# Squared-ReLU attention and feed-forward on one core: first batch split at 128 queries, score bursts joined behind v products, w_out sums on two engines

## The chip, the core and the metric

The kernel runs on one NeuronCore of a Trainium2 chip. Its engines work side by side, each through its own list of instructions in a fixed order, and wait for each other by semaphores: TensorE (matmuls and transposes, PE in the profile; PEld is its weight loads), VectorE (DVE), ScalarE (ACT), GpSimd (POOL) and SyncE (SP, which here only starts DMAs). TensorE writes to PSUM; VectorE and ScalarE carry results from there to SBUF; GpSimd works from SBUF to SBUF and also starts some DMAs. The metric is the device time of one execution in microseconds, as a median over runs.

## The reference

Attention with a squared ReLU in place of the softmax, for 8 batches, 12 heads, 448 positions and 64 dimensions a head, and then a feed-forward layer with a squared ReLU on the 3584 tokens:

```python
scores = scale * np.matmul(q, k.transpose(0, 1, 3, 2))
attn = np.maximum(scores, 0.0) ** 2 / S
attn_out = np.matmul(attn, v)
x = np.ascontiguousarray(attn_out.transpose(0, 2, 1, 3)).reshape(B * S, H * D)   # 3584 x 768
h = x @ w_in                                                                      # 768 x 2048
r = np.maximum(h, 0.0)
g = r * r
return (g @ w_out).astype(np.float32)                                             # 2048 x 768
```

## The kernel before

**Units and rounds.** A unit `n` is four heads of one batch: three units a batch, 24 in all. The 448 positions are seven groups of 64, and a round is one key group `t` of one unit. For each round four 64x64-tiled matmuls (`scores`, L379) give the scores of 448 queries against 64 keys for the unit's four heads, in a PSUM tile `sp` of which there are two. `square` carries them on in two passes: relu with a scale, PSUM to `rel` (VectorE L405 or ScalarE L408), then the square, `rel` to `at` in fp16 (ScalarE L412 or GpSimd L414). When the seven rounds of a unit are there, `av` multiplies by v (28 tiled matmuls, L442) into two `mm` banks (of four), and a copy (L462, L464) writes x, turned, so that model dimensions lie on partitions (`xt`).

**Feed-forward.** `h_mms` (L503) takes 128 columns of w_in as the weights and streams x past them, six matmuls for each of the 16 blocks of 128 rows of h; `evac_g` squares h on ScalarE (L492) and zeroes it where h was not positive on VectorE (L487). The product with w_out goes in groups of matmuls of 384 columns: the first batch partly in plain groups (`plain_groups`, L595), the rest by a Strassen-like scheme of seven products for eight (`o_groups`, L657), which needs sums of g blocks (`combine`, L636, VectorE) and sums of w_out blocks (`combine_w2`, L621): t1, t2, t4 and t3, each in two halves of 1536 elements, all on GpSimd, with the planned time 60 us as the earliest.

**The start.** Batch 0 is cut by queries, `PARTS`: 256 and 192. The scores of the first 256 queries come first, for pairs of rounds in one score tile, with their v products; then `h_pair` computes h for two blocks of 128 rows with the 256 queries, while the scores of the other 192 follow. q and k of units 0 to 5 are turned by TensorE transposes (`turn_pe`, L319), later ones by DMA transposes (`turn_dma`, L334). Loads of v, w_in and w_out go through GpSimd's DMA queue (L348, L353, L358), q and k mostly through SP's (L277). Where TensorE has nothing ready before the planned time 45 us, the planner puts in dummy matmuls (`fill`, L794).

**The order.** Nothing in the code runs in the order in which it stands. Every operation goes into a list (`plan.add`, `plan.pe`) with the engines that could do it, their costs, what it depends on, the buffers it needs and a due time. `Plan.run` then plays this list through with these costs, lets each engine take the ready operation with the earliest due time (`pick`), and so fixes each engine's order of instructions when the program is built. On the chip only the order and the true dependences are left, not the planned times. In the steady part the main loop adds two rounds of scores as one operation (a score pair, eight matmuls), now and then a v product (`avs`), and then h and w_out groups by a credit of time (`run_some`). A change between 64x64 tiles and full 128x128 matmuls has a cost in the planner (`SWITCH`).

Of the kernel before, what the change touches and what calls it, by code (L numbers as in the profile page):

```python
# [27 lines left out]
class Op:  # L28
    def __init__(self, alts, deps, bufs, due, after, mode):
        self.alts = alts  # L30
        self.bufs = bufs
        self.due = due
        self.after = after
        self.mode = mode
        self.fixed = due is not None
        self.nexts: list = []
        self.deps = [d for d in deps if d is not None]
        self.engine = None
        self.start = self.end = 0.0


class Plan:
# [29 lines left out]
    def run(self):  # L72
# [19 lines left out]
        mode, dma, done = None, 0.0, 0  # L92
        while done < n_ops:
# [6 lines left out]
            while again:  # L100
                again = False
                for eng in ("PE", "ACT", "DVE", "POOL", "SP"):
                    if self.busy[eng] > now + 1e-9:
                        continue
                    got = self.pick(eng, now, waiting)
# [10 lines left out]
                    if eng == "PE":  # L116
                        begin += self.SWITCH.get((mode, op.mode), 0.0)
# [38 lines left out]
        return max(op.end for op in self.ops)  # L156

# [35 lines left out]
def kernel(  # L193
# [117 lines left out]
    def turn_pe(n, w, cast, at=None):  # L311
        op, blk, view = cast
        ps, to = Buf("mm"), Buf("qkt")

        def flip():
            flat = ps.tile.bitcast(FP16)
            for t in range(TJ):
# [3 lines left out]
        def copy(fn):  # L321
            return lambda: fn(to.tile.rearrange("p t c -> p (t c)"),
                              ps.tile.bitcast(FP16)[:, 0:TJ * P])

        pe = plan.pe(0.4, flip, [op], [blk, ps], at=at)
        done = plan.add([("DVE", 0.55, 0.62, copy(nc.vector.tensor_copy)),
                         ("ACT", 0.82, 0.91, copy(nc.scalar.copy))], [pe], [ps, to],
                        due=plan.now + 0.3)
        qkt[n, w] = done, to

    def turn_dma(n, w, cast):
# [3 lines left out]
            out=to.tile, in_=blk.tile.rearrange("p t c -> p (t c)")))], [op], [blk, to])  # L335
        qkt[n, w] = done, to
# [26 lines left out]
    PARTS = slice(0, 4 * TP), slice(4 * TP, S)  # L363
    WHOLE = slice(0, S)

    def scores(rounds, bufs, cols, joint, at=None):
# [4 lines left out]
        def emit():  # L371
            for j, (n, t) in enumerate(rounds):
                qT, kT = qkt[n, "q"][1].tile, qkt[n, "k"][1].tile
                sp, c0 = (bufs[0].tile, j * w) if joint else (bufs[j].tile, 0)
                for e in range(2):
                    for f in range(2):
# [10 lines left out]
        return plan.pe(0.000424 * w * len(rounds), emit, [x[0] for x in turned],  # L387
                       bufs + [x[1] for x in turned], "tile", at)
# [34 lines left out]
    def av(n, ts, cols=WHOLE, at=None):  # L423
# [3 lines left out]
        joint = w < S and u == 1  # L427
        c0 = w if joint else 0
# [20 lines left out]
        op = plan.pe(0.000424 * w * len(ts), emit, [z[0] for z in used] + [vst[n][0]] + before,  # L449
                     [z[1] for z in used] + [vst[n][1]] + banks, "tile", at)  # L450
        av_ops.setdefault(n, []).append(op)
        if ts[-1] < TJ - 1 or (w < S and u == 0):
            return
        for f in range(2):
            def put(kind, f=f):
                def run():
                    dst, src = x.tile[:, 2 * u + f, cols], banks[f].tile[:, 0:w]
                    if joint:
                        dst = x.tile[:, f:f + 3:2, cols]
                        src = banks[f].tile[:, 0:2 * w].rearrange("p (u c) -> p u c", c=w)  # L460
# [6 lines left out]
            n_el = 2 * w if joint else w  # L467
            xt_ops.setdefault((b, cols.start), []).append(plan.add(
                [act(n_el, put("ACT")), dve(n_el, put("DVE"))], av_ops[n][-1:],
                [banks[f], x], due=plan.now + 0.2))  # L470

# [47 lines left out]
    def h_pair(f, cols, at=None):  # L519
        w = cols.stop - cols.start  # L520
        cost = max(0.1, 0.000424 * w) * NM
        cell: list = []

        def half(z):
            def run(at=None):
                gts.setdefault(0, Buf("g"))
                if not cell:
                    cell.append(Buf("mm"))
                op = plan.pe(cost, h_mms(cell[0], 0, f + z, cols, z * w),
                             xt_ops[0, cols.start] + [w1_ops[(f + z) // 4]] + cell[1:],  # L530
                             [cell[0], xts[0]], at=at)
                cell.append(op)
                if z:
                    evac_g(op, cell[0], 0, [f, f + 1], cols)
            return run

        return [(cost, half(z)) for z in range(2)]

    def store(op, places, cols, osb):
# [5 lines left out]
        for i, (b, t) in enumerate(places):  # L545
            ways = [("SP", 0.56, 3.0, emit(nc.sync, i, b, t))]
            if ending and len(fifo) < 7:
                ways.append(("ACT", 0.56, 3.0, emit(nc.scalar, i, b, t)))
# [62 lines left out]
    def combine_w2():  # L611
# [5 lines left out]
        for name, args, before in steps:  # L617
# [3 lines left out]
                           nc.gpsimd.tensor_sub(*args(r)))],  # L621
                         [w for hf in range(2) for w in w2_ops[hf]]
                         + [t_ops[x][z] for x in before]
                         + (plain_ops if name == "t3" else []), after=60.0)
# [115 lines left out]
    def push_dense(b):  # L740
        if b:
            hs = [h_group(b, f) for f in range(NF)]
        else:
            hs = list(first_h) + [z for f in range(0, NF, 2) for z in h_pair(f, PARTS[1])]
# [31 lines left out]
    NPE = 6  # L776
    ROUNDS = NUN * TJ
# [32 lines left out]
    w1_ops = [load_w1(0, 1.4, 1.4)]  # L810
    load_v(2, 1.4, 1.5)
# [4 lines left out]
    turn_pe(0, "k", casts[0, "k"], 5.8)  # L816
    turn_pe(0, "q", casts[0, "q"])
    rounds = [divmod(r, TJ) for r in range(STREAM)]
    tiles = [(part, rounds[r:r + 2]) for part in range(2) for r in range(0, STREAM, 2)]
    NA = len(tiles) // 2  # L820
    turns = {1: (1, "k"), 2: (1, "q"), 3: (2, "k"), 4: (2, "q")}
    first_h = deque(z for f in range(0, NF, 2) for z in h_pair(f, PARTS[0]))
# [8 lines left out]
    def some_h(count):  # L831
        for _ in range(count):
            first_h.popleft()[1]()

    def tile(i, at=None):
        part, rs = tiles[i]
# [11 lines left out]

    for i in range(NA):
        tile(i, 7.6 + 1.1 * i)  # L850
        if i >= 2:
            put(0, tiles[i - 2][1])
        if i in turns:
            n, w_ = turns[i]
            turn_pe(n, w_, casts[n, w_])
    tile(NA)
    put(0, tiles[NA - 2][1])
    tile(NA + 1)
    put(0, tiles[NA - 1][1])
# [8 lines left out]
    for i in range(NA + 2, 2 * NA):  # L868
        tile(i)
        if (i - NA) % 2:  # L870
            some_h(2)
        if i == NA + 8:
            put(1, rounds[0:2 * TJ])
            some_h(1)
    for w_ in "kq":
        turn_pe(3, w_, casts[3, w_])
    some_h(1)
    put(1, rounds[2 * TJ:])
    some_h(len(first_h))
# [4 lines left out]

# [67 lines left out]
```

## Time and profile before

| | |
|---|---|
| median of 7 runs | 394.09 us (392.44 to 394.46) |
| the profiled execution | 393.74 us, of it 392.0 us from the first to the last instruction (the span) |
| mean granted TensorE clock | 0.996 of full |
| TensorE h, 448 columns (L503) | 672 matmuls |
| TensorE w_out products (L657) | 208 + 208 + 176 + 88 + 32 + 16 matmuls of 384 columns |
| ScalarE squares (L412, 896 elements) | 104, mean 953 ns |
| GpSimd squares (L414, 896 elements) | 43, mean 1680 ns |
| GpSimd w_out sums (L621) | 8, mean 3083 to 3116 ns |
| dummy matmuls (L794) | 52 |
| w_in blocks (L353) | 4 DMAs, 768 KB each, median 13.4 us from issue to landing |

Read it so: the span is one execution on the hardware's profiler, in microseconds from its first instruction; a group is the instructions of one line and one shape, with the time its engine was busy with them and the mean time of one. Matmuls overlap, so the sum over a group is best taken from start to start in the timeline.

### The profile page before, as it was taken

What the parts mean: (1) busy time and instruction counts of PE and PEld (TensorE: products, weight loads), DVE (VectorE), ACT (ScalarE), POOL (GpSimd) and SP (SyncE); (2) the same over time, 40 slices, a digit from 0 to 9 for tenths busy, and PEclk for the clock granted to TensorE, in tenths of its full rate; (3) what the DMA queues carried; (4) which work ended last, traced back from release to release, by engine and by line L of the source; (5) the groups of instructions that cost most, each with busy time, mean ns of one, the idle gap of its engine ahead of it and who ended that gap; (6) DMA issues with size and microseconds to landing.
All of it is one profiled execution on the core that took longest, in us unless ns stands there. A gap on an engine that the chain in (4) does not pass through costs nothing.

```text
span 392.0 us, 8414 instructions
## 1 busy us (share of the span) xinstructions
PE 381.8 (97%) x3344; PEld 200.7 (51%) x3344; DVE 256.0 (65%) x362; ACT 278.8 (71%) x409; POOL 194.5 (50%) x179
## 2 busy tenths in 40 slices
PE   8999999999799999999999999999999999999995
PEld 4567765444355444544454444544545445555563
DVE  2876664476694678676886576865796567455941
ACT  3987899997866687788886787587787776244221
POOL 8577498899857574463433443175432344000100
PEclk9999999999899999999999999999999999999999
DMA  9999999962677774866397486674183001210152
GB/s 191 195 224 271 281 235 165 272 128 89 105 159 215 179 167 77 194 161 135 65 215 172 107 208 130 174 164 79 37 112 82 0 2 47 56 40 3 27 134 82
DMA packets 69671, 52.72 MB, mean 134 GB/s; under 512 B 36864, under 2 KB 69632, under 8 KB 69632
## 3 DMA queue, kind: packets, MB, share of 16 engines
q1 hardware_dynamic: 53744, 38.61, 39.0%
q0 software_dynamic: 15296, 12.72, 22.4%
q10 hardware_dynamic: 592, 0.85, 0.6%
q8 instruction: 26, 0.43, 0.4%
q14 instruction: 13, 0.11, 0.1%
HBM read 45.61 MB, written 11.01 MB: 144 GB/s over the span
## 4 chain that ended last, share of the span: by engine, by line
PE 79%; POOL 7%; ACT 5%; issue 3%; DVE 3%; DMA 1%; SPq 0%; DVEq 0%; POOLq 0%; ACTq 0%
PE mm L503 31%; PE mm L657 29%; PE sp L379 8%; PE mm L442 7%; POOL wt L621 3%; ACT at L412 2%; ACT rel L408 2%; POOL w L621 1%; DMA raw<-in_q_dram 1%; PE mm L794 1%; PE mm L791 1%; DVE rel L405 1%; DVE comb L636 1%; PE mm L319 1%; POOL at L414 1%
## 5 line engine op out<-in xcount | busy, mean ns | idle before, releaser
L503 PE MATMUL mm<-xt,w 128*128 128x448 f16 (+2 forms) x864 | 156.5, 332 | 0.8 <-DVE g L487 0.8
L414 POOL TENSOR_TENSOR at<-rel 128x896 f16<-128x896 f32 (+1 forms) x47 | 78.0, 1662 | 78.6 <-DVE rel L405 71.9
L503 PEld LDWEIGHTS <-w 128*128 128x128 f16 x864 | 79.5, 98 | 71.0 <-issue 15.2
L405 DVE TENSOR_SCALAR rel<-sp 128x896 f32<-128x896 f32 (+3 forms) x85 | 91.8, 1088 | 35.1 <-PE sp L379 27.2
L487 DVE SCALAR_TENSOR_TENSOR g<-mm,g 128x448 f16<-128x448 f32 (+2 forms) x128 | 79.0, 621 | 54.0 <-ACT g L492 53.5
L412 ACT ACTIVATE at<-rel 128x896 f16<-128x896 f32 (+2 forms) x111 | 103.3, 943 | 3.7 <-PE mm L442 1.0
L492 ACT ACTIVATE g<-mm 128x448 f16<-128x448 f32 (+2 forms) x128 | 69.1, 546 | 42.2 <-PE mm L503 40.6
L408 ACT ACTIVATE rel<-sp 128x896 f32<-128x896 f32 (+2 forms) x84 | 76.4, 912 | 12.8 <-PE sp L379 10.3
L300 POOL CAST blk<-raw 128x896 f16<-128x896 f32 x42 | 40.2, 965 | 52.0 <-issue 26.2
L657 PEld LDWEIGHTS <-comb 128*128 128x128 f16 x416 | 38.9, 98 | 32.7 <-issue 5.0
L379 PE MATMUL sp<-qkt,qkt 64*64 64x448 f16 (+2 forms) x756 | 50.3, 339 | 2.2 <-ACT rel L408 1.8
L579 ACT ACTIVATE part<-mm 128x384 f32<-128x384 f32 x46 | 22.5, 488 | 38.5 <-PE mm L657 38.3
L669 DVE SCALAR_TENSOR_TENSOR part<-mm,part 128x384 f32<-128x384 f32 x52 | 28.5, 553 | 25.9 <-ACT part L579 17.7
L657 PE MATMUL mm<-wt,comb 128*128 128x384 f16 x208 | 37.2, 327 | 0.5 <-DVE comb L636 0.5
L657 PE MATMUL mm<-w,comb 128*128 128x384 f16 x208 | 36.8, 326 | 0.0
L442 PE MATMUL mm<-at,vs 64*64 64x448 f16 (+1 forms) x672 | 35.0, 341 | 1.4 <-DVE g L487 1.4
L657 PEld LDWEIGHTS <-g 128*128 128x128 f16 x264 | 25.2, 99 | 20.9 <-issue 5.3
L657 PE MATMUL mm<-w,g 128*128 128x384 f16 x176 | 31.1, 326 | 0.0
L379 PEld LDWEIGHTS <-qkt 64*64 64x64 f16 x756 | 15.5, 105 | 29.1 <-issue 27.9
L348 POOL DMA_DIRECT2D vs<-in_v_dram x48 | 29.9, 627 | 0.4 <-DMA g<-in_q_dram 0.4
L442 PEld LDWEIGHTS <-vs 64*64 64x64 f16 x756 | 20.7, 107 | 15.4 <-issue 5.0
L561 POOL COPY rest<-g 128x1024 f16<-128x1024 f16 x8 | 9.9, 1239 | 31.8 <-DVE g L487 31.8
(48 smaller groups left out, 221.2 us busy)
## 6 DMA issues: line engine op xcount, KB each, us to landing
out_dram<-part SPq DMA_DIRECT2D x108, 96.0 KB, 2.2
raw<-in_k_dram SPq DMA_DIRECT2D x22, 448.0 KB, 4.5
raw<-in_q_dram SPq DMA_DIRECT2D x21, 448.0 KB, 4.9
vs<-in_v_dram POOLq DMA_DIRECT2D x48, 112.0 KB, 4.0
w<-in_moe_w_in_dram POOLq DMA_DIRECT2D x4, 768.0 KB, 13.4
w<-in_moe_w_out_dram POOLq DMA_DIRECT2D x4, 768.0 KB, 18.1
qkt<-blk SPq DMA_TRANSPOSE x36, 3.3
raw<-in_q_dram ACTq DMA_DIRECT2D x1, 448.0 KB, 4.9
```

The costliest lines, as they stand in the source:

```text
L300: return lambda: fn(blk.tile.rearrange("p t (f d) -> p f t d", f=2), tile_of().rearrange("p f (t d) -> p f t d", d=D))
L348: nc.gpsimd.dma_start(out=buf.tile[64 * r:64 * r + 64], in_=src[:, u, hs])
L379: nc.tensor.matmul(sp[64 * c:64 * c + 64, e, c0:c0 + w].rearrange("p (t c) -> p t c", c=TP), lhsT=kT[r, t, 64 * e:64 * e + 64], rhs=qT[r, ...
L405: dve(n, lambda: nc.vector.tensor_scalar(out=rel(), in0=sp.tile[:, :, 0:width], scalar1=0.0, scalar2=SK, op0=ALU.max, op1=ALU.mult)),
L408: act(n, lambda: nc.scalar.activation(out=rel(), in_=sp.tile[:, :, 0:width], func=AF.Relu, scale=SK))],
L412: act(n, lambda: nc.scalar.activation(out=dst(), in_=rel(), func=AF.Square)),
L414: lambda: nc.gpsimd.tensor_mul(dst(), rel(), rel()))],
L442: nc.tensor.matmul(banks[f].tile[64 * e:64 * e + 64, c0:c0 + w], lhsT=vs[r, e ^ c, t * D:(t + 1) * D], rhs=a[r, e, :], start=(t == 0), sto ...
L487: nc.vector.scalar_tensor_tensor(out=dst, in0=src, scalar=0.0, in1=dst, op0=ALU.is_gt, op1=ALU.mult)
L492: nc.scalar.activation(out=dst, in_=src, func=AF.Square)
L503: nc.tensor.matmul(bank.tile[:, c0:c0 + w], lhsT=w1[f // 4][:, m, f % 4 * P:(f % 4 + 1) * P], rhs=xts[b].tile[:, m, cols], start=(m == 0), ...
L657: nc.tensor.matmul(buf.tile[:, 0:HALF], lhsT=lhs()[:, j, :], rhs=w[:, j, :], start=(first and j == 0), stop=(j == NH - 1), skip_group_chec ...
```

## The change

1. `PARTS` becomes 128 and 320 queries. The first part's scores go four rounds to a score tile, its v products of all three units into one pair of banks. q of units 0 to 2 is turned in two parts (`turn_pe` with `ts`): the two groups that the 128 queries need, and the other five later.
2. h of the first 128 queries (`h_first`) is computed the other way round: x is the weight, 512 columns of w_in stream past it, four blocks of six matmuls; the result has queries on partitions, is squared and masked in a `comb` buffer, and is then turned by 16 TensorE transposes into g. h of the other 320 goes block by block (`h_part`).
3. A score pair becomes two operations, and each operation of a tiled burst names the next one as its `glue`: TensorE's turn is held for up to 0.45 planned us when the glued one will be ready, and it is taken first. After a v product no dense work is added before the next score pair (`MERGE`), so that pair, product and pair can stand together.
4. w_out's sums may be done by VectorE as well, and their earliest time of 60 us is dropped.
5. The planner charges DMA time for stores and DMA transposes. V of unit 2 is loaded ahead of w_in's first block.

```diff
@@ Plan.run
+                    got = None
+                    if eng == "PE" and last is not None and last.glue is not None:
+                        soon = self.soon(last.glue)
+                        if now < soon <= now + 0.45:
+                            heapq.heappush(events, soon)
+                            continue
+                        if soon <= now:
+                            got = waiting.index((last.glue.due, last.glue.id, last.glue)), (
+                                last.glue.alts[0])
+                    got = got or self.pick(eng, now, waiting)
...
+    def soon(self, op):
+
+        if op.wait or op.engine:
+            return 1e9
+        at, need = op.ready, {}
+        for b in op.bufs:
+            if b.tile is None:
+                need[b.pool] = need.get(b.pool, 0) + 1
+        for pool, k in need.items():
+            slots = sorted(x[0] for x in self.pools[pool])
+            at = max(at, slots[k - 1] if len(slots) >= k else 1e9)
+        return at
@@ turn_pe, turn_dma
-    def turn_pe(n, w, cast, at=None):
+    def turn_pe(n, w, cast, at=None, ts=range(TJ)):
...
-        done = plan.add([("SP", 1.3, 5.0, lambda: nc.sync.dma_start_transpose(
-            out=to.tile, in_=blk.tile.rearrange("p t c -> p (t c)")))], [op], [blk, to])
+        done = plan.add([("SP", 1.3, 5.0, lambda: nc.sync.dma_start_transpose(
+            out=to.tile, in_=blk.tile.rearrange("p t c -> p (t c)")), 1000000)], [op], [blk, to])
@@
-    PARTS = slice(0, 4 * TP), slice(4 * TP, S)
+    PARTS = slice(0, 2 * TP), slice(2 * TP, S)
@@ h
+    def h_first():
+
+        work = []
+        for two in range(2):
+            buf, marks = Buf("comb"), []
+
+            def wide(z, i, buf=buf, marks=marks):
+                def run():
+                    bank = Buf("mm")
+
+                    def emit():
+                        for m in range(NM):
+                            nc.tensor.matmul(
+                                bank.tile, lhsT=xts[0].tile[:, m, PARTS[0]], rhs=w1[i][:, m, :],
+                                start=(m == 0), stop=(m == NM - 1), skip_group_check=True)
...
+                    op = plan.pe(0.2157 * NM, emit, xt_ops[0, 0] + [w1_ops[i]], [bank, xts[0]])
+                    one = plan.add([act(512, lambda: nc.scalar.activation(
+                        out=dst(), in_=bank.tile, func=AF.Square))], [op], [bank, buf],
+                        due=plan.now + 0.3)
+                    marks.append(plan.add([dve(512, mask)], [one], [bank, buf],
+                                          due=plan.now + 0.9))
+                return run
+
+            def turn(two=two, buf=buf, marks=marks):
...
+                    for f in range(NH):
+                        nc.tensor.transpose(flat[:, f * P:(f + 1) * P], buf.tile[:, f], ident)
...
+            work += [(0.2157 * NM, wide(z, 2 * two + z)) for z in range(2)]
+            work.append((0.057 * NH, turn))
+        return work
@@ store
-            ways = [("SP", 0.56, 3.0, emit(nc.sync, i, b, t))]
+            ways = [("SP", 0.56, 3.0, emit(nc.sync, i, b, t), 98304)]
@@ combine_w2
                            lambda r=slice(4 * z, 4 * z + 4), args=args:
-                           nc.gpsimd.tensor_sub(*args(r)))],
+                           nc.gpsimd.tensor_sub(*args(r))),
+                          ("DVE", 0.9, 0.98,
+                           lambda r=slice(4 * z, 4 * z + 4), args=args:
+                           nc.vector.tensor_sub(*args(r)), 0, True)],
...
-                         + (plain_ops if name == "t3" else []), after=60.0)
+                         + (plain_ops if name == "t3" else []))
@@ push_dense
-            hs = list(first_h) + [z for f in range(0, NF, 2) for z in h_pair(f, PARTS[1])]
+            hs = [z for f in range(NF) for z in h_part([f], PARTS[1])]
@@ start
-    w1_ops = [load_w1(0, 1.4, 1.4)]
-    load_v(2, 1.4, 1.5)
+    load_v(2, 1.4, 1.4)
+    w1_ops = [load_w1(0, 1.4, 1.5)]
...
+    quads = [rounds[r:r + 4] for r in range(0, STREAM, 4)]
+    turn_pe(0, "k", casts[0, "k"], 5.6)
+    turn_pe(0, "q", casts[0, "q"], None, QA)
+    for i, rs in enumerate(quads):
+        tile(0, rs, 7.0 + 1.2 * i)
+        if i in (0, 1):
+            turn_pe(i + 1, "k", casts[i + 1, "k"])
+            turn_pe(i + 1, "q", casts[i + 1, "q"], None, QA)
+        if i:
+            put(0, quads[i - 1])
+    for n in range(NU):
+        turn_pe(n, "q", casts[n, "q"], None, QB)
@@ main loop
-        bufs = [Buf("s") for _ in rs]
-        op = scores(rs, bufs, WHOLE, False)
-        for sp, (n, t) in zip(bufs, rs):
+        todo = []
+        for n, t in rs:
+            sp = Buf("s")
+            op = scores([(n, t)], [sp], WHOLE, False)
+            todo.append((op, sp, n, t))
+            if chain is not None:
+                chain.glue = op
+            chain = op
+        for op, sp, n, t in todo:
             second, at = square(op, sp, S)
             ats[n, t] = second, at, lambda tl: tl
         if i in avs:
-            av(avs[i], list(range(TJ)))
+            chain.glue = av(avs[i], list(range(TJ)))
+            chain = chain.glue
         if i in pushes:
             push_dense(pushes[i])
+        if i in avs and MERGE and i + 1 < NB:
+            skipped = 1
+            continue
         nxt = min([j for j in pushes if j > i] or [NB + 2])
-        run_some(max(0.0, (queued - 4.0) / (nxt - i)))
+        run_some(max(0.0, (queued - 4.0) * (1 + skipped) / (nxt - i + skipped)))
+        skipped, chain = 0, None
```

## The prediction

> **What bounds the kernel now.** I read the busy shares first, then the stretches, then TensorE's timeline where it stops.
>
> ```profile
> PE 381.8 (97%) x3344; PEld 200.7 (51%) x3344; DVE 256.0 (65%) x362; ACT 278.8 (71%) x409; POOL 194.5 (50%) x179
> ```
>
> TensorE is the bound over the whole, so a change counts by the TensorE time it removes, or by the stops it ends. Stretches of the same trace (PE, weight loads, VectorE, ScalarE, GpSimd, then clock, DMA share, GB/s):
>
> ```profile
> 50.00:55.00 5.00, 4.67 (x76) 2.81 (x69) 3.63 (x5) 5.00 (x9) 5.00 (x5) 1.00 1.30 203
> 60.00:70.00 10.00, 10.00 (x95) 5.12 (x93) 4.04 (x5) 9.88 (x15) 8.05 (x8) 1.00 1.22 192
> 102.00:104.00 2.00, 0.54 (x5) 0.14 (x5) 0.00 (x0) 2.00 (x3) 2.00 (x4) 1.00 0.33 63
> 104.00:106.00 2.00, 1.15 (x20) 0.82 (x23) 1.83 (x3) 1.75 (x3) 2.00 (x2) 0.89 0.97 139
> 106.00:108.00 2.00, 2.00 (x15) 0.77 (x8) 2.00 (x3) 1.62 (x3) 0.65 (x1) 0.50 1.06 177
> 108.00:110.00 2.00, 2.00 (x11) 1.07 (x10) 2.00 (x4) 0.60 (x1) 0.00 (x0) 0.76 1.02 381
> ```
>
> From 50 to 70 ScalarE is full while VectorE is about half idle. At 102 to 106 TensorE stops, and for 6 us after it has a lower clock. TensorE's timeline (start, us, operation, idle before):
>
> ```profile
> 26.12 2.79 PE L503 MATMUL mm<-xt,w 128*128 128x256 f16 x24
> ...
> 41.96 0.38 PE L379 MATMUL sp<-qkt,qkt 64*64 64x448 f16 x4
> ...
> 57.75 2.77 PE L595 MATMUL mm<-w,g 128*128 128x384 f16 x16
> ...
> 77.67 0.57 PE L379 MATMUL sp<-qkt,qkt 64*64 64x448 f16 x8
> 78.17 1.31 PE L503 MATMUL mm<-xt,w 128*128 128x448 f16 x6
> 79.41 0.57 PE L379 MATMUL sp<-qkt,qkt 64*64 64x448 f16 x8
> ...
> 102.92 0.38 PE L379 MATMUL sp<-qkt,qkt 64*64 64x448 f16 x4 [1.00 <-ACT rel L408]
> 103.11 0.35 PE L442 MATMUL mm<-at,vs 64*64 64x448 f16 x1
> 104.85 2.18 PE L442 MATMUL mm<-at,vs 64*64 64x448 f16 x27 [1.39 <-DVE g L487]
> ...
> 173.88 0.57 PE L379 MATMUL sp<-qkt,qkt 64*64 64x448 f16 x8
> 174.28 1.49 PE L442 MATMUL mm<-at,vs 64*64 64x448 f16 x28
> 175.70 3.58 PE L503 MATMUL mm<-xt,w 128*128 128x448 f16 x18
> ```
>
> Three landmarks carry the sum: unit 3's first score at 41.96, the first w_out group at 57.75, TensorE's end at 388.0. Behind 57.75 the idle pieces are 0.41, 0.37, 1.00, 1.39, 0.38 and 0.16: 3.7 us. The lowered clock costs 2 x (0.11 + 0.50 + 0.24) = 1.7. So 5.4 of the last 330.25 us is not work.
>
> **The sums on VectorE.** On GpSimd, w_out's eight half sums take 3.1 us each between 62 and 98, 24.8 us in all. Meanwhile its squares go to ScalarE, which is full. The stop at 102 follows: ScalarE's relu there waited 1.26 us for a GpSimd square. In the built order GpSimd keeps three halves (9.3 us) and VectorE gets five. The nearest row for one is VectorE's fp16 sum of 1024 elements, 0.68 us, started 0.60 apart; 1536 elements make 0.9, five 4.5, in stretches where VectorE is busy 4.04 of 10 us. Beside GpSimd's work such a sum took longer:
>
> ```profile
> 109.47 0.68 DVE L636 TENSOR_TENSOR comb<-g,comb 128x1024 f16<-128x1024 f16 x1
> ...
> 110.74 1.34 DVE L636 TENSOR_TENSOR comb<-g 128x1024 f16<-128x1024 f16 x1
> ```
>
> The second ran beside a GpSimd cast of 0.93. Scaled, five sums are 4.5 to 10 us. The first stands on VectorE ahead of the masks of the last two h blocks, and the first w_out group waits for these. The bounds of this delay are 0 and one GpSimd half sum, 3.1; I take 0, since the nearest wait (1.34 - 0.68 = 0.66) fits into the slack behind the joined burst that TensorE runs there. Dropping the 60 us due time puts no early load wait in: the built first sum waits for two w_out blocks, and the later landed at 36.1 + 17.3 = 53.4; the second sum needs the last block (39.45 + 21.8 = 61.2), and VectorE gets there some groups later.
>
> One rule speaks against this edit. The Trainium skill, "SBUF — State Buffer", section "SBUF: two separate sides", says a VectorE operation with two SBUF inputs and a GpSimd operation that reads SBUF exclude each other for a whole instruction. The 1.34 us row agrees with it, and by the rule the forecast below would be 3.1 us longer if the two halves of the first sum started together.
>
> So I count the stops at 82 to 107 as gone: of the 5.4 us, 0.54 (behind 330 us) stay, and I add 1.0 for new ones, 1.5 together; bounds 0.5 to 5.4. Gain 3.9.
>
> **The joined bursts.** TensorE changes between 64x64 tiles and full matmuls. A score pair takes 0.40 before a v product (173.88 to 174.28) and 0.50 before h (77.67 to 78.17); a v product 1.42 before h and 1.35 before scores (156.97 to 158.32 in the trace). Six h matmuls take 1.135 in a row of h and 1.24 between two tile bursts (78.17 to 79.41), 0.105 more. Pair, product, h, pair costs 0.40 + 1.42 + 0.505; joined, 0.40 + 1.35 + 0.505, and one 0.105 falls away too: 0.18 a burst. Counted in the built orders, behind the first w_out group 68 bursts become 54: 14 x 0.18 = 2.5 us. Its cover is that the second pair finds its score buffers free. It comes 0.40 + 1.35 = 1.75 us behind the first; at 77.67 and 79.41 pairs stood 1.74 apart with no idle time, ScalarE full. Without that cover see the rivals. A planner hold of up to 0.45 us is no wait on the chip, where only order remains.
>
> **The start.** The h matmuls cost the same: before, 96 x 0.1095 (24 in 26.12 to 28.85 less 0.105) + 96 x 0.082 (18 in 42.28 to 43.87) = 18.4. After, 24 of 512 columns, estimated at 0.216 from the 0.1625 of 384 and 0.189 of 448 columns, 5.2; 96 of 320 at 0.137 (between 0.1095 and 0.1625), 13.1; 16 turns at 0.06 (seven in 0.39 to 0.49), 0.9. Total 19.2. What moves is when. ScalarE's list from its first relu (9.61): 8 passes of 1024 at 0.93 and 4 of 640 at 0.61 (768 take 0.72 apart, slope 0.82 ns an element) give x of the 128 at 19.4. V's third load, now ahead of w_in's first block, costs nothing, as both landed by 18.7. Then 12 passes of 640, 3 squares of 512 at 0.5 and x copies of 0.75: 29. There TensorE reaches w_in's fourth block. In the trace it was issued at 13.86 and landed 19.3 us later, at 33.2, with DMA share over 1.1 throughout; the same bytes are ahead of it, so it lands there again and TensorE waits about 3 us, longer than the stop at 102. Then 6 matmuls 1.3, square 0.6, mask 0.7, four handovers of 0.2, and 15 turns 0.95 give 37.5; half clock behind the wait 1.0: unit 3's scores at 38.5 (36 to 41). More dummy matmuls (62, were 52) fill only empty places; if late, 0.11 each. Query turns in two parts add a 0.15 start per copy, on engines that have room there.
>
> From 38.5: scores 0.40, the last v product of 320 at 0.96, three turns of seven 1.35, a half pair 0.4, h 13.1, four lone pairs 2.44 and two joined bursts 4.56: 23.2, so w_out's first group starts at 61.7. By then three score rounds and a v product (0.6 + 1.35) more than before are done: the same place before is 59.7. The start loses 2.0; bounds, from 36 and 41: a gain of 0.5 and a loss of 4.5.
>
> The loads' and stores' number is unchanged. The planner's new prices for transposes and stores only reorder SP's queue; raw loads precede their casts by over ten us, which hides it; without, a cast is late by a transpose's issue, 1.3.
>
> **Sum.** 61.7 + (330.25 - 5.4 - 1.95 - 2.5) + 1.5 = 383.6; the tail behind TensorE (388.0 to 392.0) 4.0: span 387.6. The profiled run took 393.74 for its 392.0, 1.74 around: 389.35. It lay 0.35 under the median of 394.09: **389.7**.
>
> **Rivals.**
> A, more: w_in lands at 31 or the passes are faster, scores at 36, waits 0.5 instead of 1.5: 389.7 - 2.5 - 1.0 = 386.2. For it: the passes of 640 are only interpolated. Against: DMA was full.
> B, handed back: VectorE's first sum meets GpSimd's (3.1) and half clock follows, or scores start at 41: 389.7 + 2.5 to 4.8, 392.2 to 394.5. For it: the 1.34 row. Against: GpSimd has casts there, not always sums.
> C, slower: the joined bursts starve. Four score tiles reach two engines within 2.3 us where each relu takes 0.92 to 1.09; if each of 15 such bursts finds ScalarE in one more pass (0.95), 14.3 us: 404.0. It decides from (394.9 - 389.7) / 15 = 0.35 us a burst. For it: only two score buffers; ScalarE full at 60 to 80. Against: the 1.74 row, and ScalarE is busy 30.24 of 40 us from 240 on.
> D, the order does not join: excluded by the built order, 15 bursts are pair, product, pair.
>
> **Chances.** Forecast 0.45, A 0.2, B 0.2, C 0.15. What can be told apart is 0.2%, 0.8 us: 393.3 to 394.9. B reaches half into it: faster 0.76, same 0.09, slower 0.15. The range runs from A to B's end, 386.0 to 394.4; the forecast's own is 388 to 391.
>
> **What would show it.** Right: no TensorE idle at 100 to 107 and clock 1.00 there; unit 3's scores near 38.5 and w_out's first group near 62; a TensorE wait before the fourth 512-column block; pairs behind v products with no idle. Wrong: many idle pieces of 0.3 us or more before scores (C), masks late behind VectorE's first w_out sum (B), or scores at 36 (A).

## The result and the profile after

The changed kernel takes 396.71 us (median of 14 runs, 395.62 to 399.0) beside 394.09 (35 runs) for the kernel before: ratio 1.0077, 95% interval 1.0059 to 1.0095. By the ratio it is 3.0 us slower, by the two medians 2.6; the forecast was 389.7, and the range ended at 394.4. The profiled execution took 396.22 us for a span of 394.3. The executions of one kernel lie up to 4 us apart, and the mean clock differs among them (in gps_half_late from 0.993 to 1.000), so what is said below of stops and of the clock holds for the profiled executions, while the ratios go by all runs.

Two lines of the page of the changed kernel: busy time of the engines, and the granted TensorE clock in 40 slices of 9.9 us.

```profile
PE 381.9 (97%) x3298; PEld 202.1 (51%) x3298; DVE 267.2 (68%) x382; ACT 279.7 (71%) x417; POOL 175.7 (45%) x174
...
PEclk9999997899999999999999999999999999999999
```

The work went where it was meant to go: GpSimd is busy for 18.8 us less, VectorE for 11.2 more. TensorE is busy as long as before, although by the forecast 14 bursts fewer need 2.5 us less, and the lowered clock has moved from the eleventh slice to the seventh and eighth. That is where TensorE's timeline has to be read (start, us, operation, idle before and its releaser):

```profile
34.01 1.46 PE L582 MATMUL mm<-w,xt 128*128 128x512 f16 x6 [0.21 <-DMA w<-in_moe_w_in_dram]
...
38.39 0.57 PE L406 MATMUL sp<-qkt,qkt 64*64 64x448 f16 x8
...
66.08 5.28 PE L682 MATMUL mm<-w,g 128*128 128x384 f16 x16 [3.80 <-DVE g L517]
71.29 0.57 PE L406 MATMUL sp<-qkt,qkt 64*64 64x448 f16 x8
71.79 2.77 PE L682 MATMUL mm<-w,g 128*128 128x384 f16 x16
```

The landmarks of the start are where the forecast put them: unit 3's first score at 38.39 (38.5), and the first w_out group would have begun at 66.08 - 3.80 = 62.28 (61.7). But TensorE waits 3.80 us there for VectorE's mask, and then runs the group in 5.28 us; the same 16 matmuls take 2.77 one group later. Windows of the same trace around the stop (PE, weight loads, VectorE, ScalarE, GpSimd, clock, DMA share, GB/s):

```profile
60.00:62.00 2.00, 1.69 (x40) 0.93 (x32) 2.00 (x1) 2.00 (x4) 2.00 (x4) 1.00 1.20 279
62.00:64.00 2.00, 0.28 (x4) 0.10 (x3) 2.00 (x1) 1.52 (x2) 2.00 (x1) 1.00 1.28 171
64.00:66.00 2.00, 0.00 (x0) 0.00 (x0) 2.00 (x3) 0.00 (x0) 0.80 (x1) 0.61 1.13 275
66.00:68.00 2.00, 1.92 (x7) 0.89 (x7) 2.00 (x5) 0.54 (x1) 0.92 (x1) 0.50 1.26 104
68.00:70.00 2.00, 2.00 (x8) 0.96 (x7) 1.49 (x2) 0.89 (x2) 0.69 (x1) 0.50 0.83 164
70.00:72.00 2.00, 2.00 (x15) 0.61 (x14) 0.57 (x2) 0.68 (x2) 2.00 (x4) 0.68 0.20 19
```

From 62.28 to 66.08 TensorE stands still, and VectorE is full with a few long instructions. Behind it the clock costs 2 x (0.50 + 0.50 + 0.32) = 2.6 us. So one place costs 3.80 + 2.6 = 6.4 us. VectorE's and GpSimd's timelines say what was ahead of the mask:

```profile
59.48 6.15 DVE L711 TENSOR_TENSOR wt<-w,w 128x1536 f16<-128x1536 f16 x1
65.55 0.88 DVE L517 SCALAR_TENSOR_TENSOR g<-mm,g 128x320 f16<-128x320 f32 x2
```

```profile
57.81 2.69 POOL L325 CAST blk<-raw 128x896 f16<-128x896 f32 x3
60.43 1.25 POOL L375 DMA_DIRECT2D vs<-in_v_dram  x2
61.68 3.12 POOL L708 TENSOR_TENSOR wt<-w,w 128x1536 f16<-128x1536 f16 x1
66.06 0.92 POOL L325 CAST blk<-raw 128x896 f16<-128x896 f32 x1 [1.25 <-DMA qkt<-blk]
```

VectorE's first w_out sum is recorded for 6.15 us, where the same sum of 1536 elements takes 0.95 with nothing beside it. It begins beside GpSimd's casts and ends 0.83 us after GpSimd's own half sum, at 61.68 + 3.12 = 64.80. The two masks that w_out's first group needs (65.55) stand behind it in VectorE's list. Its inputs were not late: the later of the two w_out blocks that it adds was issued at 40.15 and landed 16.6 us later, at 56.7. GpSimd's half sum, which in the built order waits for that block alone, was ready as well.

Behind that group little is lost: idle pieces of 1.37 us in all, the largest 1.0 at 116.20. At 100 to 107, where the kernel before stopped, there is neither idle time nor a lowered clock. Landmarks of all kernels of this study, read from TensorE's timeline as above (us; the idle time is that behind the first w_out group):

| kernel | first 448-column score | first w_out group | TensorE's end | idle behind |
|---|---|---|---|---|
| before | 41.96 | 57.75 | 387.99 | 3.71 |
| after | 38.39 | 66.08 | 390.35 | 1.37 |
| sums_late_66 | 38.5 | 62.32 | 386.66 | 3.79 |
| sums_late_no_join | 38.37 | 61.63 | 387.76 | 3.29 |
| first_sum_vector_only | 38.53 | 62.35 | 383.82 | 1.17 |
| gps_half_late | 40.06 | 63.91 | 387.42 | 3.05 |
| sums_gpsimd_60 | 39.56 | 63.39 | 383.68 | 0.43 |
| sums_gpsimd_free | 40.03 | 63.86 | 383.94 | 0.16 |
| old_sums_late | 41.74 | 57.53 | 387.00 | 4.51 |
| old_start_join | 42.05 | 59.3 | 382.17 | 0.31 |
| join_only | 41.74 | 58.99 | 383.42 | 2.12 |
| prices_only | 41.98 | 57.77 | 384.45 | 1.78 |

### The profile page after: what moved, and what is told of

It is laid out like the page before. It is cut to its first block, busy times and chain, and to the rows that moved or that the text cites. A ratio compares the mean times of both kernels' runs of the same rounds, so it can differ in the third digit from the quotient of the medians.

```text
span 394.3 us, 8331 instructions
## 1 busy us (share of the span) xinstructions
PE 381.9 (97%) x3298; PEld 202.1 (51%) x3298; DVE 267.2 (68%) x382; ACT 279.7 (71%) x417; POOL 175.7 (45%) x174
## 4 chain that ended last, share of the span: by engine, by line
PE 82%; DMA 7%; ACT 3%; DVE 3%; issue 2%; POOL 1%; POOLq 0%; DVEq 0%
PE mm L533 36%; PE mm L747 28%; PE sp L406 8%; PE mm L471 6%; DMA w<-in_moe_w_in_dram 6%; PE mm L682 3%; DMA g<-in_q_dram 2%; DVE comb L726 1%; ACT rel L436 1%; ACT g L522 1%; ACT at L440 1%; DVE g L517 1%; POOL g L315 1%; PE mm L345 1%; DVE rel L433 0%
## 5 line engine op out<-in xcount | busy, mean ns | idle before, releaser
L533 PE MATMUL mm<-xt,w 128*128 128x448 f16 (+1 forms) x768 | 149.0, 346 | 0.0
L440 ACT ACTIVATE at<-rel 128x896 f16<-128x896 f32 (+1 forms) x120 | 109.7, 931 | 9.8 <-DVE rel L433 5.3
L517 DVE SCALAR_TENSOR_TENSOR g<-mm,g 128x448 f16<-128x448 f32 (+1 forms) x128 | 76.4, 604 | 52.3 <-ACT g L522 52.1
L533 PEld LDWEIGHTS <-w 128*128 128x128 f16 x768 | 72.3, 98 | 69.8 <-issue 11.4
L522 ACT ACTIVATE g<-mm 128x448 f16<-128x448 f32 (+1 forms) x128 | 67.1, 534 | 41.3 <-PE mm L533 40.5
L436 ACT ACTIVATE rel<-sp 128x896 f32<-128x896 f32 (+2 forms) x87 | 78.0, 900 | 9.0 <-PE sp L406 7.2
L406 PE MATMUL sp<-qkt,qkt 64*64 64x448 f16 (+2 forms) x756 | 51.7, 339 | 0.8 <-DVE rel L433 0.4
L666 ACT ACTIVATE part<-mm 128x384 f32<-128x384 f32 x44 | 21.5, 488 | 41.0 <-PE mm L747 38.0
L406 PEld LDWEIGHTS <-qkt 64*64 64x64 f16 x756 | 17.3, 105 | 28.1 <-issue 24.8
L471 PEld LDWEIGHTS <-vs 64*64 64x64 f16 x756 | 22.3, 106 | 13.6 <-issue 4.2
```

What stands on the lines that cost most here:

```text
L406: nc.tensor.matmul(sp[64 * c:64 * c + 64, e, c0:c0 + w].rearrange("p (t c) -> p t c", c=TP), lhsT=kT[r, t, 64 * e:64 * e + 64], rhs=qT[r, ...
L436: act(n, lambda: nc.scalar.activation(out=rel(), in_=sp.tile[:, :, 0:width], func=AF.Relu, scale=SK))],
L440: act(n, lambda: nc.scalar.activation(out=dst(), in_=rel(), func=AF.Square)),
L471: nc.tensor.matmul(banks[f].tile[64 * e:64 * e + 64, c0:c0 + w], lhsT=vs[r, e ^ c, t * D:(t + 1) * D], rhs=a[r, e, :], start=(t == 0), sto ...
L517: nc.vector.scalar_tensor_tensor(out=dst, in0=src, scalar=0.0, in1=dst, op0=ALU.is_gt, op1=ALU.mult)
L522: nc.scalar.activation(out=dst, in_=src, func=AF.Square)
```

## The experiments

Ratios are to the kernel before, run beside each kernel on the same chip (its medians on the three chips: 393.68, 393.36 and 393.08).

### The first sum: its place, and what GpSimd holds ready

**sums_late_66**: the changed kernel, with an earliest planned time of 66 us for all w_out sums.

```diff
-                         + (plain_ops if name == "t3" else []))
+                         + (plain_ops if name == "t3" else []), after=66.0)
```

> The change with one number added: w_out's sums have 66 us of planned time as their earliest, so that VectorE's first half sum stands behind the masks of the last two h blocks. Theory (port): in the changed kernel that sum was in VectorE's list ahead of the two masks and took 6.15 us beside GpSimd's work, TensorE stopped 3.80 us and then lost 2.6 us to a lowered clock. Then here TensorE does not stop before w_out's first group, and the time is 396.7 - 6.4 = 390.3, between 389 and 392. Rival (loads): the last masks or w_out blocks are late in any case, by the DMAs of the start; then a stop of over 2 us stays at that place and the time is 394 to 397.

Measured: 393.31 us (12 runs), ratio 1.0001 (0.9979 to 1.0023), span 390.6, clock 1.0. The stop ahead of the first w_out group is gone (62.32, no idle), and so is the half clock in the profile; by the ratios that is worth 3.0 us of time. But the expected 390.3 was missed by 3.0, since TensorE now stops elsewhere. Its timeline, VectorE's and GpSimd's:

```profile
74.16 0.38 PE L406 MATMUL sp<-qkt,qkt 64*64 64x448 f16 x4 [1.25 <-DVE rel L433]
...
80.36 0.38 PE L406 MATMUL sp<-qkt,qkt 64*64 64x448 f16 x4 [1.36 <-DVE rel L433]
```

```profile
66.61 3.30 DVE L711 TENSOR_TENSOR wt<-w,w 128x1536 f16<-128x1536 f16 x2
69.83 3.28 DVE L711 TENSOR_TENSOR wt<-w,wt 128x1536 f16<-128x1536 f16 x2
73.03 1.08 DVE L433 TENSOR_SCALAR rel<-sp 128x896 f32<-128x896 f32 x1
...
76.09 3.20 DVE L711 TENSOR_TENSOR wt<-wt,w 128x1536 f16<-128x1536 f16 x1
79.22 1.08 DVE L433 TENSOR_SCALAR rel<-sp 128x896 f32<-128x896 f32 x1
...
81.87 0.95 DVE L711 TENSOR_TENSOR w<-w,w 128x1536 f16<-128x1536 f16 x1
```

```profile
69.05 3.25 POOL L325 CAST blk<-raw 128x896 f16<-128x896 f32 x2
...
75.39 3.09 POOL L708 TENSOR_TENSOR w<-w,w 128x1536 f16<-128x1536 f16 x1 [0.95 <-PE mm L682]
```

Each stop is a relu behind a VectorE sum, and each long sum lies beside GpSimd work: four took 6.58 us together, 1.64 on average, and one 3.20, ending 0.81 after GpSimd's sum of 75.39. The sum at 81.87, with nothing beside it, took 0.95. GpSimd pays too: its two casts of some 0.93 took 3.25. The place of the first sum is only the worst of several.

**first_sum_vector_only**: the first sum (both halves) on VectorE alone, in the same place; the others as in the changed kernel.

```diff
-                plan.add([("POOL", 3.06, 3.1,
+                plan.add([("POOL" if name != "t1" else "none", 3.06, 3.1,
```

> The change, but both halves of the first w_out sum (t1) may only go to VectorE; the first stays in its place ahead of the two masks. Port theory: GpSimd's own half sum of 3.12 us is no longer beside it, only its casts and the start of a load, so VectorE's sum ends by 62.6 instead of 65.6, TensorE's stop shrinks from 3.80 to 1.5 or less, and the time is 391 to 394. Load rival (the sum waits for a w_out block that lands late): the sum ends at 65.6 as before, time 396 to 397.

Measured: 391.07 us (6 runs), ratio 0.9937 (0.9907 to 0.9967), span 387.8, clock 1.0. VectorE's and GpSimd's timelines at the same place:

```profile
59.62 1.84 DVE L711 TENSOR_TENSOR wt<-w,w 128x1536 f16<-128x1536 f16 x1
61.38 0.88 DVE L517 SCALAR_TENSOR_TENSOR g<-mm,g 128x320 f16<-128x320 f32 x2
```

```profile
57.95 2.69 POOL L325 CAST blk<-raw 128x896 f16<-128x896 f32 x3
60.57 1.25 POOL L375 DMA_DIRECT2D vs<-in_v_dram  x2
61.81 3.14 POOL L708 TENSOR_TENSOR wt<-w,wt 128x1536 f16<-128x1536 f16 x1
```

The sum, the casts and the load issues stand as in the changed kernel, to 0.15 us. Only GpSimd's next operation differs: here it adds to what VectorE is making, and so must wait for it. The sum takes 1.84 instead of 6.15: 1.0 behind the casts and 0.84 of its own. The w_out group begins at 62.35 without idle time. A late load as the cause is ruled out. The price of the place comes out too: by the ratios this kernel is 5.5 us faster than the changed one, of the 6.4 counted above. The time is at the lower end of what was expected, as TensorE's stop went entirely.

**gps_half_late**: the halves of the first sum divided as in the changed kernel, but by rule: the first half on VectorE, the second on GpSimd and planned not before 64 us.

```diff
-                plan.add([("POOL", 3.06, 3.1,
+                plan.add([("none" if (name, z) == ("t1", 0) else "POOL", 3.06, 3.1,
...
-                          ("DVE", 0.9, 0.98,
+                          ("none" if (name, z) == ("t1", 1) else "DVE", 0.9, 0.98,
...
-                         + (plain_ops if name == "t3" else []))
+                         + (plain_ops if name == "t3" else []), after=64.0 * ((name, z) == ("t1", 1)))
```

> The changed kernel with the first group's second half sum on GpSimd alone and planned not before 64 us; the first half is on VectorE alone, in the same place ahead of the two masks. Theory (VectorE's sum took 6.15 us because GpSimd had an independent half sum to run behind its casts): VectorE's sum takes 1 to 2.5 us at about 60 us, no TensorE stop before the first w_out group, 389 to 391.5 us. Rival (VectorE's sum is slow wherever it meets the casts and the load issues): about 6 us again, a stop of over 3 us before the first w_out group, 395 to 397 us.

Measured: 392.95 us (12 runs), ratio 0.9994 (0.9974 to 1.0014), span 391.4. VectorE and GpSimd:

```profile
61.17 1.83 DVE L711 TENSOR_TENSOR wt<-w,w 128x1536 f16<-128x1536 f16 x1
```

```profile
59.49 2.70 POOL L325 CAST blk<-raw 128x896 f16<-128x896 f32 x3
62.12 1.25 POOL L375 DMA_DIRECT2D vs<-in_v_dram  x2
63.37 3.14 POOL L708 TENSOR_TENSOR wt<-w,wt 128x1536 f16<-128x1536 f16 x1
66.43 3.12 POOL L708 TENSOR_TENSOR wt<-w,w 128x1536 f16<-128x1536 f16 x1
```

Again 1.83 us, and no stop ahead of the w_out group; here too GpSimd's next sum adds to what VectorE is making (wt<-w,wt), and its independent one comes behind that. So it is GpSimd's independent half sum, ready behind the casts and issues, that makes the sum long. The time is above what the theory gave, for two reasons that are not this sum: w_in's fourth block made TensorE wait 2.20 at 35.69, and a relu behind VectorE's sums at 71.43 and 73.00 (1.64 and 2.66) stopped it for 1.86 at 76.71.

### Who ended the old stop

**sums_gpsimd_60** and **sums_gpsimd_free**: the changed kernel with all sums on GpSimd, with the old earliest time of 60 us and without one.

```diff
-                          ("DVE", 0.9, 0.98,
-                           lambda r=slice(4 * z, 4 * z + 4), args=args:
-                           nc.vector.tensor_sub(*args(r)), 0, True)],
...
-                         + (plain_ops if name == "t3" else []))
+                         + (plain_ops if name == "t3" else []), after=60.0)
```

The last two lines are in sums_gpsimd_60 alone.

> The change with w_out's sums as before: all eight half sums on GpSimd, not before 60 us of planned time. Port theory: no sum on VectorE ahead of the masks, no stop before w_out's first group; but GpSimd is full again from 62 to 98 and part of the old stop at 82 to 107 (5.4 us with its lowered clock) comes back: 390.3 to 395.0. If the sums on VectorE are worth what the prediction said (3.9), 394; if the new order hides them, 390.5.

> The change with w_out's sums on GpSimd alone and without an earliest time. Against sums_gpsimd_60 only the dropped 60 us differ. Theory: dropping it costs nothing, as the sums wait only for blocks that have landed (56.7 and 61.7 in the changed kernel): 388 to 390. Rival (loads): GpSimd stands at a block that has not landed, its casts and squares come late, 391 or more.

Measured: 389.18 us (4 runs), ratio 0.9901 (0.9869 to 0.9932), and 388.99 (6 runs), 0.9894 (0.9871 to 0.9917). The old stop doesn't come back, so the 390.3 to 395.0 expected of sums_gpsimd_60 was missed: behind the first w_out group TensorE is idle for 0.43 and 0.16 us, less than with VectorE's help. The earliest time is worth nothing. Against the changed kernel's ratio of 1.0077, the sums on VectorE cost 0.018 x 394 = 7.2 us (sums_gpsimd_free; the other kernel gives 6.9).

**old_sums_late**: the kernel before with sums on VectorE too, from 66 us, and nothing else.

```diff
-                           nc.gpsimd.tensor_sub(*args(r)))],
+                           nc.gpsimd.tensor_sub(*args(r))),
+                          ("DVE", 0.9, 0.98,
+                           lambda r=slice(4 * z, 4 * z + 4), args=args:
+                           nc.vector.tensor_sub(*args(r)), 0, True)],
...
-                         + (plain_ops if name == "t3" else []), after=60.0)
+                         + (plain_ops if name == "t3" else []), after=66.0)
```

> The kernel before with one part alone: w_out's sums also on VectorE, from 66 us on. The prediction's term: the old stop at 82 to 107 goes, 3.9 us less, 389.8. Rival (port): each sum of 0.9 beside GpSimd's work takes 1.5 to 3.3 us, VectorE's relus behind it come late and TensorE stops for score buffers at 66 to 82 as it did for 2.6 us in the kernel with the sums at 66 us; then 392 to 394.

Measured: 392.64 us (12 runs), ratio 0.9982 (0.9964 to 1.0001). The stop at 102 is gone, but idle time behind the group is 4.51 instead of 3.71, in other pieces. The largest, from TensorE's, VectorE's and GpSimd's timelines:

```profile
77.85 1.48 PE L503 MATMUL mm<-xt,w 128*128 128x448 f16 x7 [1.66 <-DVE xt L464]
```

```profile
71.81 5.45 DVE L624 TENSOR_TENSOR w<-w,w 128x1536 f16<-128x1536 f16 x2
77.19 0.61 DVE L464 TENSOR_SCALAR xt<-mm 128x448 f16<-128x448 f32 x1
```

```profile
71.45 1.24 POOL L300 CAST blk<-raw 128x896 f16<-128x896 f32 x1 [1.23 <-DMA raw<-in_q_dram]
72.66 3.79 POOL L621 TENSOR_TENSOR wt<-wt,w 128x1536 f16<-128x1536 f16 x1
```

The same picture without any other part of the change: two VectorE sums take 5.45 us (1.68 and 3.85) beside a cast and a GpSimd sum, and end 0.8 after it (72.66 + 3.79 = 76.45); x, behind them, is late.

**join_only** and **prices_only**: the kernel before with the joined bursts alone, and with the planner's DMA prices alone.

```diff
-            out=to.tile, in_=blk.tile.rearrange("p t c -> p (t c)")))], [op], [blk, to])
+            out=to.tile, in_=blk.tile.rearrange("p t c -> p (t c)")), 1000000)], [op], [blk, to])
...
-            ways = [("SP", 0.56, 3.0, emit(nc.sync, i, b, t))]
+            ways = [("SP", 0.56, 3.0, emit(nc.sync, i, b, t), 98304)]
...
-                ways.append(("ACT", 0.56, 3.0, emit(nc.scalar, i, b, t)))
+                ways.append(("ACT", 0.56, 3.0, emit(nc.scalar, i, b, t), 98304))
```

This is prices_only; join_only is item 3 of the change.

> The kernel before with one part of the change alone: the score bursts joined behind v products, without the planner's new prices for stores and transposes; all w_out sums on GpSimd as before. Theory (the joined bursts ended TensorE's stops at 82 to 107 us): no half-clock stretch there, 387 to 389 us, ratio to before 0.984 to 0.990. Rival (the new prices ended them): the stops stay, and only the joined bursts' 2.3 us are gained, 391 to 392.5 us.

> The kernel before with the planner's new prices for stores and transposes alone, no joined bursts. Theory (the joined bursts ended the stops): the stops or their like stay between 70 and 110 us, 393 to 394.5 us. Rival (the new prices ended them): no half-clock stretch at 82 to 107 us, 389 to 391 us.

Measured: join_only 389.38 us (7 runs), ratio 0.9913 (0.9883 to 0.9943); prices_only 390.11 (6 runs), 0.9922 (0.9903 to 0.9941). Neither profile shows the half clock, so my theory is wrong for the prices: alone they gain 3.1 us. join_only lies just above the theory's range, with one stop of 1.79 left, at 106.34. It is behind a VectorE sum of g blocks, which all these kernels have, and which took 3.79 us; the same sum of 1024 elements took 0.68 in the kernel before at 109.47. It began beside two load issues on GpSimd and ended 0.57 behind the copy and the square that followed them:

```profile
102.50 3.79 DVE L661 TENSOR_TENSOR comb<-g 128x1024 f16<-128x1024 f16 x1
```

```profile
101.86 1.18 POOL L373 DMA_DIRECT2D vs<-in_v_dram  x2
103.03 1.06 POOL L586 COPY rest<-g 128x1024 f16<-128x1024 f16 x1
104.03 1.69 POOL L439 TENSOR_TENSOR at<-rel 128x896 f16<-128x896 f32 x1
```

GpSimd's timelines tell how the prices end the old stop, the kernel before first:

```profile
61.97 3.13 POOL L621 TENSOR_TENSOR wt<-w,w 128x1536 f16<-128x1536 f16 x1
...
68.89 0.93 POOL L300 CAST blk<-raw 128x896 f16<-128x896 f32 x1 [1.77 <-DMA qkt<-blk]
71.18 0.93 POOL L300 CAST blk<-raw 128x896 f16<-128x896 f32 x1 [1.36 <-DMA raw<-in_q_dram]
...
95.05 3.08 POOL L621 TENSOR_TENSOR wt<-wt,w 128x1536 f16<-128x1536 f16 x1
...
100.21 1.71 POOL L414 TENSOR_TENSOR at<-rel 128x896 f16<-128x896 f32 x1
```

```profile
62.00 6.18 POOL L621 TENSOR_TENSOR wt<-w,w 128x1536 f16<-128x1536 f16 x2
...
91.87 3.09 POOL L621 TENSOR_TENSOR wt<-wt,w 128x1536 f16<-128x1536 f16 x1
...
97.05 1.70 POOL L414 TENSOR_TENSOR at<-rel 128x896 f16<-128x896 f32 x1
```

Before, two casts wait 1.77 + 1.36 = 3.1 us for DMAs, with seven half sums and the squares queued behind them. With the prices the planner expects these DMAs later and puts the second half sum ahead of the casts; those waits are gone, GpSimd's work from the sixth half sum on is 3.2 us earlier, and the square that ScalarE's relu waited for before 101.95 starts at 97.05 instead of 100.21. In the built orders TensorE's, VectorE's and ScalarE's lists are the same in both kernels up to about 103 us, so the stop was ended by the lists of SP and GpSimd. How the joined bursts alone, without these prices, got rid of it was not followed up.

### The joined bursts, the start, and the best kernel

**sums_late_no_join**: sums_late_66 without joining.

```diff
-    MERGE = True
+    MERGE = False
...
-                chain.glue = op
+                pass
...
-            chain.glue = av(avs[i], list(range(TJ)))
-            chain = chain.glue
+            av(avs[i], list(range(TJ)))
```

> The same as the kernel with the sums at 66 us, but with no joined bursts: no hold for the next tiled operation, and dense work goes in behind a v product again. The prediction's term: 14 bursts more at 0.18 us, so 2.5 us longer than the kernel with the sums at 66 us, 392.8 by the theory. Rival (starving): the joined pairs wait for score buffers, then this one is as fast or faster than the joined one, 390 or less.

Measured: 394.2 us (12 runs), ratio 1.0018 (1.0001 to 1.0036). From the first w_out group to TensorE's end, less idle time, it takes 387.76 - 61.63 - 3.29 = 322.8 us; sums_late_66 takes 386.66 - 62.32 - 3.79 = 320.6. Of this difference of 2.3 us, 0.4 is two rounds of scores that sums_late_66 has done ahead of its first group. The other 1.9 goes with the bursts: behind the first group the traces have 65 without joining and 54 with it, so 11 fewer, at 0.17 each. (Without joining, six bursts in the trace still are pair, product and pair, so 11 bursts go and not the 14 expected.) In time only 0.9 shows between the medians, and 0.7 by the ratios, as the two differ in stops and start as well; the expected 2.5 was missed.

**old_start_join**: the kernel before with joined bursts and prices; the start and GpSimd's sums from 60 us stay. Its edit is item 3 of the change with the diff of prices_only.

> The kernel before with the joined bursts and the planner's new prices alone: its own start (256 and 192 queries), w_out's sums on GpSimd from 60 us on. Beside the kernel with sums_gpsimd_60 it differs in the start alone, beside the kernel before in the bursts alone. By the prediction's sum the new start loses 2.0 us, and by the traces w_out's first group is at 63.4 there against 57.75 + 2.0 here: then 389.2 - 2.0 to 3.7 = 385.5 to 387.2. Rival (the new start pays): 389.2 or more. Against the kernel before, the bursts' 2.5 us give 391.2 if the old stop at 82 to 107 stays, and 386 if the new order has lost it.

Measured: 387.81 us (5 runs, 387.6 to 388.11), ratio 0.9864 (0.9836 to 0.9891), idle time behind the group 0.31. This is the fastest kernel of the study, ahead of both, though 0.6 above the 385.5 to 387.2 that was expected. It differs from sums_gpsimd_60 by the new start alone, which therefore costs (0.9901 - 0.9864) x 394 = 1.5 us, and by TensorE's ends 383.68 - 382.17 = 1.5. By the intervals of the two ratios the 1.5 is uncertain by about as much.

## Why the prediction was wrong

The kernels form a chain in which each has one part more than the one ahead of it, and the ratios price each step: the planner's prices -3.1 us (prices_only), joined bursts -2.3 (old_start_join), the start +1.5 (sums_gpsimd_60), the dropped 60 us -0.3 (sums_gpsimd_free), the sums on VectorE +7.2 (the changed kernel). That they add up to the +3.0 of the whole is no test, as the chain ends at the changed kernel; and by the intervals each step is uncertain by 0.7 to 1.6 us. The price of a part also depends on its company: the joined bursts are worth 3.4 us alone (join_only), where they end most of the old stop, 2.3 behind the prices, and 0.7 with the sums on VectorE. The sums on VectorE stand out by far in any case.

**The step that failed** is "The bounds of this delay are 0 and one GpSimd half sum, 3.1; I take 0". The place and the mechanism were named, in rival B and in the last sign of "wrong", but the price taken and its bound were too small. The wait held the sum not for one GpSimd instruction: casts 1.0, two load issues 1.2, the half sum 3.1, and its own 0.83, together 6.15. The slack ahead of the masks, which I counted on, took about 2.3 of this; 3.80 reached TensorE, and the half clock added 2.6. The row I reasoned from (1.34 beside a cast) had GpSimd busy for 0.93. The same trace, of the kernel before, had a longer wait, 4.3 us ahead of the rows that I showed (VectorE's and GpSimd's timelines):

```profile
105.18 2.03 DVE L636 TENSOR_TENSOR comb<-g 128x1024 f16<-128x1024 f16 x1
```

```profile
104.94 1.71 POOL L414 TENSOR_TENSOR at<-rel 128x896 f16<-128x896 f32 x1
```

This sum of 0.68 waited 1.35 for a whole GpSimd square and ended 0.56 behind it (107.21 and 106.65). So the "nearest wait" of 0.66 was that of a short GpSimd instruction; behind a half sum of 3.1 the same reading gives a wait of about 3, an estimate from these two rows, and more than the slack there was. The rule weighed there (the Trainium skill, "SBUF — State Buffer", section "SBUF: two separate sides") has the two engines exclude each other for a whole instruction. The runs agree: the sums of 6.15 and 3.20 us, and the second of the two that took 5.45, all end some 0.8 us after GpSimd's. By the rule the forecast would have been 3.1 longer, 392.8, nearer than with the 0 that I took, and still short, as a cast, two load issues and the half sum all went first. The five sums on VectorE together took 10.0 us, the upper end of the 4.5 to 10 that I allowed (my own scaling gives 8.9 there, not 10); what cost time was the place of the first.

**Rival B** was therefore the case, with a price of 6.4 instead of 2.5 to 4.8, which put it out of the range. Put into the sum, it closes: first group 62.28 instead of 61.7, + 3.80 + 2.6, idle time behind 1.37 instead of 1.5: 383.6 + 0.6 + 6.4 - 0.1 = 390.5 for TensorE's end, measured 390.35.

**"The sums on VectorE ... Gain 3.9"** was credited to the wrong part. The stops at 82 to 107 are gone as forecast, but with all sums on GpSimd they are gone too, so that the size of this term came out right is luck. The sums alone on VectorE gain 0.7 us (ratio 0.9982, an interval that touches 1). I read the stop as GpSimd having too much to do and ScalarE being full; GpSimd was late by two waits for DMAs in its own list, and without these the stop at 102 went with all eight half sums still on GpSimd (prices_only).

**"The planner's new prices ... only reorder SP's queue"** is wrong: they reorder GpSimd's list and are worth 3.1 us by themselves. I costed the edit by the cover of the raw loads, "over ten us", and did not compare GpSimd's list. There one of the two late casts waited for a transpose's buffer (1.77 us at 68.89), and the other for its raw load (1.36 at 71.18), which had been issued at 65.45, so the cover was less than six.

**The joined bursts** were right: 0.17 us a burst measured, 0.18 forecast, and the 54 bursts are there; 14 of them make 2.4 us of TensorE work, 2.5 forecast. There is no starving (rival C): in the changed kernel scores behind v products have no idle time. Rival D is out as well, with 15 bursts of pair, product and pair in the trace.

**The start** was right in its landmarks, and it costs 1.5 where 2.0 was forecast. Of its terms, the wait for w_in's fourth block was over-sized: about 3 us forecast (by its own times, 33.2 - 29, it is 4.2), 0.21 in the changed kernel, and 0.48 to 2.20 in the six others with this start. The passes before it were slower: TensorE came to the fourth block at 33.8, not 29. That the first score came at 38.39 beside 38.5 is in part luck: the block let TensorE go on at 34.0 instead of 33.2, and the 1.0 us of half clock behind the wait did not come (the clock is 1.00 from 32 to 40 us), two errors that cancel.

**Rival A** did not happen: the scores began at 38.39, not 36.

## What to carry to other kernels

Where two engines exclude each other, optional work on the one must not stand in its in-order list ahead of something urgent while the other has a run of such work ready: price it by the whole run of it, not by one instruction. A stop that names a busy engine may come from that engine's own waits earlier on: read its list back for idle time with a DMA as releaser before moving its work to another engine. And an edit of a planner's price changes every engine's list, so compare all lists and test each part alone before crediting a gain.

## What the runs showed of the hardware

- VectorE's fp16 sum of 1536 elements took 0.95 us alone, up to 3.9 beside GpSimd work, and 6.15 in front of a GpSimd sum that was ready. The load issues on GpSimd let VectorE's sum in at 60.6 and 62.1 us (first_sum_vector_only, gps_half_late), but not at 60.5 in the changed kernel, nor the sum of g blocks at 102.5 in join_only. That GpSimd's next, ready sum decides is shown by the first three, in two of which that next sum had to wait for VectorE's, and the fourth fits, as a ready copy stood behind its load issues; how it already holds VectorE off while loads are being issued, the records don't show, and it stays open.
- GpSimd is lengthened too: a square 2.32 for 1.67, two casts 3.25 for 1.86, a half sum 3.79 for 3.1.
- The clock fell during TensorE's 3.80 us of waiting (0.61 from 64 to 66 us) and stayed at 0.50 for some 4 us and 0.68 for two more. Single stops of 1.66 to 2.20 us left it at 1.00 in the profiled executions (old_sums_late, join_only, gps_half_late), while 1.00 + 1.39, which ended within 2 us of each other in the kernel before, lowered it. This gives no limit: other executions of join_only and gps_half_late had a mean clock down to 0.993, and their stops were not recorded.
